# Three chunks of a fused convolution-plus-MLP kernel fed by a pre-turned copy of the input instead of transposes on TensorE, with three smaller moves in the same schedule

## The chip, the cores and the metric

The kernel runs on one core of a Trainium2 chip. The metric is device time in microseconds (us), as a median over runs. A profiled execution gives the trace: five engines (TensorE, called PE for its matmuls and PEld for its weight loads; VectorE, DVE; ScalarE, ACT; GpSimd, POOL; SyncE, SP, which only issues DMAs), each of which runs its own instructions in program order and waits on semaphores, and the DMA queues. SP and ACT issue DMAs through hardware queues, GpSimd through a software queue.

## What is computed

The input is one sequence of 2048 rows and 448 columns. All is in 32-bit floats.

```python
xn  = layernorm(q)                                  # per row
# branch A: a gated long convolution
k_s = sum over t of shift(k, t) * shift_k[:, 3 - t] # 4 taps, per column
kv  = k_s * v
y   = causal_conv(kv, ssm_k) + kv * ssm_D           # 2048 taps per column, by FFT
# branch B: an MLP
h   = xn @ w1 + b1                                  # 448 -> 1792
out = q + xn * y + mish(h) @ w2                     # 1792 -> 448
```

## The kernel before

**Precision by splitting.** Every float operand of the MLP is split in two: `hi = round(x)` by a cast on ACT and `lo = x - hi` by a subtraction on DVE. Each product is then three matmuls (hi*hi, hi*lo, lo*hi) at the fast matmul rate.

**MLP slots.** The 2048 rows are 8 chunks (`NCHUNK`) of 256 rows; the 1792 hidden columns are 7 pairs of 128 (`NP`). There are 56 (chunk, pair) steps `i`, and every step has two slots. In slot 2i PE does `g1_mm(i)` (L444: 22 matmuls of 256 columns). In slot 2i+1 ACT and DVE do `mish(i)` (L460: two activations, then the split into `ach`, `acl`), and PE does `g2_mm(i-2)` (L472: 12 matmuls of 448 columns). Chunk c begins in slot 14c. `g2_evac` (L486) adds the finished chunk to its rows of q and stores them.

**What feeds a chunk.** `g1_mm` needs the normalized rows with the 448 columns on partitions. For chunk c+1 this is made while chunk c runs: `ln_load` (L363) loads q, `ln_stats` (L400) takes mean and variance on DVE, the power -0.5 on POOL and `xn = (q - mean) * rstd` on POOL (on DVE for chunks 0 and 7); `ln_T` (L421) has PE turn xn with four 128x128 transposes for each half chunk, against an identity matrix, into a PSUM tile; `x_split` (L413) makes the two halves `XH` (ACT) and `XL` (DVE). The halves come in slots 2(7c+5)+1 and 2(7c+6) of the chunk before. The xn tile has one buffer. Statistics are put in a list, `drip`, from which one item is taken after most DVE operations (`dv`).

**The convolution** is a two-step FFT by matmuls, dealt out over the same slots by a plan that is written out by hand (`at(slot, ...)` runs ahead of the slot's MLP work, `after(slot, ...)` behind it, L91 to L95).
- Slots 1 to 60: `f1_mm` (L118: 16 matmuls in row and column tiles) for 8 groups of the filter h (`H_AT`; one group, `H_HEAD`, goes in slot 1) and 8 groups of kv (`KV_AT`). It needs both buffers of PSUM pool `pc`. `f1_fold` (L128) empties them with one ACT copy and two DVE operations into an `st` tile (2 buffers), and `f1_out` (L137) has ACT issue two DMAs of `st` to the scratch `Dh` or `Dkv` in DRAM. Ahead of each kv group come four `taps` on DVE (L157; one product on POOL), which end with the product by v (L175).
- Slots 63 to 90: eight octets. `o_load` (L189) loads `ah` from Dh and `av` from Dkv on SP's queue (one buffer each, so each load waits for the matmuls that read the octet before); `h2_mm`, `v2_mm`, `prod`, `i1_mm` transform, multiply and transform back; every one of them needs both `pc` buffers, so the ACT copies of the one before must be done. The load of `av` for octet 0 needs all groups of Dkv to have landed.
- Slots 92 to 112: `e_load`, `fold`, `i2_mm`, `gate`: the last transform and the product with xn. Chunks 6 and 7 (`LATE`) are gated ahead of their MLP sum, the others are added to the output by a DMA.

**The head.** The weights w1 and w2 are loaded and split while chunk 0 runs (`w1_load` L335, `w1_split` L349, `w2_load` L353, `w2_split` L357; raw tiles `kr`, 4 buffers), so that PE takes up each piece soon after it lands. In slot 4 the plan has `f1_mm` of h's group 2 ahead of `g1_mm(2)`, in slot 8 that of group 3. The constant `f1id` holds the first transform's matrix and the identity in one load (L607).

Of the kernel before, what the change touches and what calls it, by code (L numbers as in the profile page):

```python
# [7 lines left out]
F32 = mybir.dt.float32  # L8
# [17 lines left out]
H_AT = {2: 4, 3: 8, 0: 12, 4: 16, 5: 20, 6: 26, 7: 32}  # L26
KV_AT = (24, 29, 34, 39, 44, 50, 55, 60)
# [5 lines left out]
T_LATE = 5  # L33
# [5 lines left out]
def tile_kernel(ctx: ExitStack, tc, q, k, v, sk, hT, sD, w1, b1, w2, c_f1, c_g, c_gi, c_i2, out):  # L39
# [18 lines left out]
    E = dp.tile([NJ * 4, 64, D], F32, name="E")  # L58

    f1id = cp.tile([128, 2, 128], F32, name="f1id")  # L60
    f1, ident = f1id[:, 0], f1id[:, 1]
# [4 lines left out]


# [50 lines left out]
    def f1_mm(src, g, key):  # L118
        x = src.pop(g)
        PS[key, g] = ps = [pc(), pc()]  # L120
        for b in range(2):
            for h in range(2):
                for jj in range(2):
                    rg = 32 * (2 * b + h)
                    nc.tensor.matmul(ps[h][64 * jj:64 * jj + 64, b, :D], f1[rg:rg + 32, 0:64], x[rg:rg + 32, jj],  # L125
                                     start=True, stop=True, tile_position=(rg, 64 * jj))
# [10 lines left out]
    def f1_out(dst, g, key):  # L137
        st = ST.pop((key, g))
        for jj in range(2):
            nc.scalar.dma_start(dst.rearrange("(h p) n d -> p h n d", h=2)[:, :, 4 * g + 2 * jj:4 * g + 2 * jj + 2].rearrange("p h n d -> p h (n d)"),  # L140
                                st[64 * jj:64 * jj + 64].rearrange("p h b d -> p h (b d)"))
# [170 lines left out]
    def gate(c):  # L312
        p = PS.pop(("P", c))
        for jj in range(2):
            j = 2 * c + jj
            r = rstd[:, j:j + 1]
# [44 lines left out]
    XS, XN, turned = {}, {}, []  # L361
# [8 lines left out]

    def ln_parts(c):
        st = mp.tile([128, 2, 6], F32, name="bst", bufs=2)
        ve = mp.tile([128, 2], F32, name="ve", bufs=2)
        xn = mp.tile([128, 2, D + 64], F32, name="xn", tag="xn", bufs=1)
        XN[c] = xn
        eng = nc.gpsimd if 0 < c < NCHUNK - 1 else V

        def stats(jj):
            V.bn_stats(st[:, jj], Q[c][:, jj])

        def aggr(jj):
            V.bn_aggr(mv[:, 2 * c + jj], st[:, jj])

        def eps(a, b):
            V.tensor_scalar(ve[:, a:b], mv[:, 2 * c + a:2 * c + b, 1], EPS, None, op0=ALU.add)  # L385

        def power(a, b):
            nc.gpsimd.tensor_tensor(rstd[:, 2 * c + a:2 * c + b], ve[:, a:b], mhalf[:, a:b], op=ALU.pow)  # L388

        def norm(jj):  # L390
            j = 2 * c + jj
            eng.tensor_scalar(xn[:, jj, :D], Q[c][:, jj], mv[:, j, 0:1], rstd[:, j:j + 1],  # L392
                              op0=ALU.subtract, op1=ALU.mult)

        def tail(a, b):
            eng.tensor_copy(xn[:, a:b, D:], xn[:, a:b, D - 64:D])
# [24 lines left out]
    def ln_T(c, jj):  # L421
# [64 lines left out]
    def g2_evac(c, jjs=(0, 1)):  # L486
# [6 lines left out]
        if not late(c):  # L493
            nc.sync.dma_start(out[:, 2 * c:2 * c + 2], x)

    def mlp_slot(s):
# [3 lines left out]
        if half == 0:  # L500
            if i < n:
                c, p = pairs[i]
                if c + 1 < NCHUNK:
                    if p == 0:
                        ln_load(c + 1)
                    if p == (3 if c in (0, 2, NCHUNK - 2) else 2):
                        ln_stats(c + 1)
# [5 lines left out]
        else:  # L513
            if i < n:
                c, p = pairs[i]
                if p == NP - 2 and c + 1 < NCHUNK:
                    ln_T(c + 1, 0)
# [12 lines left out]
    for g, t in H_AT.items():  # L530
# [8 lines left out]
        at(t + 3, f1_out, Dh, g, "h")  # L539
# [4 lines left out]
    for g, t in enumerate(KV_AT):  # L544
# [9 lines left out]
        at(t + 3, f1_out, Dkv, g, "kv")  # L554
# [34 lines left out]

    at(ts[0] - 7, lambda: dv(len(drip)))  # L590

# [3 lines left out]
    wz = cp.tile([128, NJ], F32, name="wz")  # L595
# [3 lines left out]
    for _ in range(WARM):  # L599
        nc.tensor.matmul(warm[0:NJ, 0:WARM_N], wz, wz[:, 0:1].to_broadcast([128, WARM_N]), start=True, stop=True)  # L600
# [35 lines left out]
    plan.setdefault(4, []).insert(0, (f1_out, (Dh, H_HEAD, "h")))  # L636
    for s in range(nslots):
# [10 lines left out]
        turn()  # L648
# [7 lines left out]
def _constants():  # L656
# [29 lines left out]
    return dict(c_f1=c(np.stack([f1, np.eye(128)], axis=1)), c_g=c(G.reshape(128, 8, 4, 2, 32)), c_gi=c(GI.reshape(128, 8, 2, 2, 64)),  # L686
# [28 lines left out]
```

## Time and profile before

| what | value |
|---|---|
| median of 3 runs | 369.38 us (369.35 to 369.51) |
| profiled execution: its own time | 370.86 us |
| its span, first to last instruction | 368.9 us |
| PE busy | 360.9 us (98%) |
| DVE busy | 262.5 us (71%) |
| ACT busy | 166.3 us (45%) |
| POOL busy | 71.2 us (19%) |
| granted TensorE clock | 1.000 |
| DMA | 79.35 MB, mean 215 GB/s |

The profiled execution's time is 1.96 us more than its span (what lies ahead of the first and behind the last instruction) and 1.48 us more than the median. A row of the timeline reads: start, duration, engine, line, operation, tile written<-tiles read, count, and in brackets the idle time of the engine ahead of it with what ended that time. Rows of a group (by line and form) give the busy time, the mean duration of one in ns, and the idle time ahead. The ends of matmuls are modelled: what PE really took for one is read from start to start.

### The profile page before, as it was taken

To read this page: it belongs to the slowest core of one execution; us is meant where nothing else is said; L and a number is where in the kernel's file an instruction comes from. 1 tells how busy PE (TensorE), PEld (TensorE's weight loads), DVE (VectorE), ACT (ScalarE), POOL (GpSimd) and SP (SyncE) were. 2 spreads that over 40 slices of the span, in tenths; PEclk is the share of its full clock that TensorE was granted. 3 is DMA by queue.
4 is the path that set the end of the run, shared out by engine and by line. 5 is a ranking of instruction groups with operands and counts; after the bars stand their busy time and mean duration, and the time that the engine had idled before them with its cause. 6 is when DMAs were issued, how large, how long until landed. Compare 5 with 4: busy or idle time off the path is not lost.

```text
span 368.9 us, 7464 instructions
## 1 busy us (share of the span) xinstructions
PE 360.9 (98%) x3128; PEld 292.6 (79%) x3128; DVE 262.5 (71%) x359; ACT 166.3 (45%) x277; POOL 71.2 (19%) x58
## 2 busy tenths in 40 slices
PE   7998999999999999999999999999999999999995
PEld 2697888978888989889868666666666889889885
DVE  5897858999998888996515657656385752897751
ACT  3757543344241443253254555556655533235450
POOL 2005000920228222611006000060000005102020
PEclk9999999999999999999999999999999999999999
DMA  7998996839496329514675598896694375949655
GB/s 241 346 285 312 358 368 184 256 105 295 105 299 214 89 66 274 170 48 101 225 244 174 194 261 238 282 301 189 209 292 125 95 248 205 419 195 276 116 66 133
DMA packets 32354, 79.35 MB, mean 215 GB/s; under 512 B 2881, under 2 KB 19138, under 8 KB 32322
## 3 DMA queue, kind: packets, MB, share of 16 engines
q1 hardware_dynamic: 20210, 44.09, 35.8%
q10 hardware_dynamic: 9776, 22.88, 22.2%
q0 software_dynamic: 2336, 11.93, 11.3%
q8 instruction: 24, 0.39, 0.4%
q14 instruction: 8, 0.07, 0.1%
HBM read 50.44 MB, written 28.44 MB: 214 GB/s over the span
## 4 chain that ended last, share of the span: by engine, by line
PE 71%; DMA 12%; DVE 9%; POOL 3%; ACT 2%; issue 2%; SPq 0%; ACTq 0%; POOLq 0%; DVEq 0%
PE pg L457 27%; PE pg L482 10%; PE pg L484 9%; PE pg L483 9%; PE pc L208 7%; DMA kr<-in_w_dram 6%; PE pc L251 4%; PE pc L125 2%; PE pc L308 2%; DMA Dh<-st 2%; DVE x L172 2%; PE pg L407 2%; POOL xn L392 2%; DMA Dkv<-st 1%; DMA av<-Dkv 1%
## 5 line engine op out<-in xcount | busy, mean ns | idle before, releaser
L465 ACT ACTIVATE a<-pg,b1t 128x256 f32<-128x256 f32 x112 | 47.1, 472 | 113.0 <-PE pg L457 88.2
L457 PE MATMUL pg<-XH,w1h 128*128 128x256 f32 x448 | 91.3, 285 | 0.9 <-ACT XH L419 0.9
L75 DVE TENSOR_TENSOR acl<-a,ach 128x512 fp32r<-128x512 f32 x56 | 38.8, 693 | 65.0 <-ACT ach L74 64.7
L457 PEld LDWEIGHTS pg<-XH,w1h 128*128 128x128 f32 x448 | 69.6, 188 | 18.9 <-issue 15.7
L482 PE MATMUL pg<-w2h,ach 128*128 128x448 f32 x224 | 83.1, 371 | 0.0
L483 PE MATMUL pg<-w2l,ach 128*128 128x448 f32 x224 | 81.3, 363 | 0.9 <-DVE w2l L75 0.9
L484 PE MATMUL pg<-w2h,acl 128*128 128x448 f32 x224 | 81.4, 363 | 0.0
L457 PE MATMUL pg<-XL,w1h 128*128 128x256 f32 x448 | 69.6, 277 | 0.2 <-DVE XL L417 0.2
L457 PEld LDWEIGHTS pg<-XL,w1h 128*128 128x128 f32 x448 | 59.4, 188 | 0.4 <-DVE XL L417 0.4
L457 PE MATMUL pg<-XH,w1l 128*128 128x256 f32 x336 | 56.8, 277 | 0.0
L482 PEld LDWEIGHTS pg<-w2h,ach 128*128 128x128 f32 x224 | 42.0, 188 | 11.7 <-issue 9.4
L457 PEld LDWEIGHTS pg<-XH,w1l 128*128 128x128 f32 x336 | 46.8, 188 | 0.0
L483 PEld LDWEIGHTS pg<-w2l,ach 128*128 128x128 f32 x224 | 42.1, 188 | 3.6 <-DVE w2l L75 1.2
L484 PEld LDWEIGHTS pg<-w2h,acl 128*128 128x128 f32 x224 | 42.1, 188 | 2.5
L388 POOL TENSOR_TENSOR rstd<-ve,mhalf 128x2 f32<-128x2 f32 (+1 forms) x9 | 8.8, 977 | 156.2 <-DVE ve L385 156.1
L74 ACT CAST ach<-a 128x512 fp32r<-128x512 f32 x56 | 34.7, 620 | 1.8
L155 POOL TENSOR_TENSOR x<-kr,skb 128x896 f32<-128x896 f32 x8 | 17.1, 2133 | 83.6 <-DVE x L154 62.4
L392 POOL TENSOR_SCALAR xn<-qt,mv,rstd 128x448 f32<-128x448 f32 x12 | 27.8, 2320 | 0.6
L172 DVE TENSOR_TENSOR x<-x 128x896 f32<-128x896 f32 x24 | 26.8, 1115 | 1.4 <-POOL x L155 0.9
L131 ACT COPY st<-pc 128x896 f32<-128x896 f32 x16 | 14.5, 906 | 14.5 <-PE pc L125 12.6
L132 DVE TENSOR_TENSOR st<-pc,st 128x896 f32<-128x896 f32 x16 | 17.4, 1088 | 3.6 <-ACT st L131 3.1
L259 ACT COPY qe<-pc 128x896 f32<-128x896 f32 x16 | 13.8, 912 | 11.0 <-PE pc L251 10.8
(70 smaller groups left out, 389.7 us busy)
## 6 DMA issues: line engine op xcount, KB each, us to landing
Dh<-st ACTq DMA_DIRECT2D x16, 448.0 KB, 6.4
Dkv<-st ACTq DMA_DIRECT2D x16, 448.0 KB, 5.1
ah<-Dh SPq DMA_DIRECT2D x8, 896.0 KB, 7.0
av<-Dkv SPq DMA_DIRECT2D x8, 896.0 KB, 6.2
E<-qe ACTq DMA_DIRECT2D x16, 448.0 KB, 5.2
e<-E POOLq DMA_DIRECT2D x8, 896.0 KB, 7.9
kr<-in_k_dram SPq DMA_DIRECT2D x10, 448.0 KB, 6.7
x<-in_v_dram SPq DMA_DIRECT2D x8, 448.0 KB, 5.2
```

The source lines that it names most:

```text
L74: nc.scalar.copy(h, raw)
L75: V.tensor_sub(l, raw, h)
L132: V.tensor_add(st[:, 0], e, st[:, 1])
L155: nc.gpsimd.tensor_mul(o, KR[g - u // 2], skb[:, u:u + 1].to_broadcast([128, 2, D]))
L172: V.tensor_add(KV[g], KV[g], o)
L208: nc.tensor.matmul(p[32 * t:32 * t + 32, r, :D], g[rs, t, c], a[rs, t], start=True, stop=True, tile_position=(64 * r, 32 * t))
L392: eng.tensor_scalar(xn[:, jj, :D], Q[c][:, jj], mv[:, j, 0:1], rstd[:, j:j + 1], op0=ALU.subtract, op1=ALU.mult)
L457: nc.tensor.matmul(ps[:, n], l, r, start=n_ == 0, stop=n_ == len(mm) - 1)
L465: nc.scalar.activation(a[:, n], ps[:, n], AF.Mish, bias=b1t[:, 2 * p + n:2 * p + n + 1])
L482: nc.tensor.matmul(ps, ah[:, n, cs], w2h[:, f], start=f == 0, stop=False)
L483: nc.tensor.matmul(ps, ah[:, n, cs], w2l[:, f], start=False, stop=False)
L484: nc.tensor.matmul(ps, al[:, n, cs], w2h[:, f], start=False, stop=f == NF - 1)
```

## The change

For chunks 5 to 7 (`NT` = 5 on) the host hands in a second copy of q, `qT`, with columns on partitions. Its 512 KB a chunk are loaded straight into the xn tile. Mean and rstd are taken from the row layout as before (rstd now overwrites the variance in `mv`); POOL stores the 256 pairs (mean, rstd) of a chunk to a DRAM tile `MR`; SP loads them back for each half chunk as one row spread over all 128 partitions, into `idr`, a tile of one buffer which held the identity; DVE subtracts the means and multiplies by rstd along the free dimension, two operations a half chunk; then the split as before, with SBUF as the source. The 24 transposes of these chunks, and POOL's (DVE's for chunk 7) normalizations of them, are gone. `NT_AT` gives the slots, counted from slot 14(c-1) (57 for c = 5).

The rest: the last kv group's `f1_mm` goes from slot 60 to 59, its store from 63 to 61, and the first load of `ah` from ahead of slot 61 to behind slot 59; h's groups 2 and 3 go one slot later (5 and 9), and the stores of groups 1, 2 and 3 are issued by GpSimd instead of ACT; the output store of chunks 0 to 5 is issued behind the next slot (`g2_out`); `f1` and the identity are two loads, the identity (64 KB) first, f1 (32 KB, half of the old columns) behind h's first group; the statistics' tail does norm and tail of a half chunk before the other half's.

```diff
-H_AT = {2: 4, 3: 8, 0: 12, 4: 16, 5: 20, 6: 26, 7: 32}
-KV_AT = (24, 29, 34, 39, 44, 50, 55, 60)
+H_AT = {2: 5, 3: 9, 0: 12, 4: 16, 5: 20, 6: 26, 7: 32}
+KV_AT = (24, 29, 34, 39, 44, 50, 55, 59)
 POOL_H = {20: (0, 2)}
 H0_AT = 63
 OCT_AT = (65, 3)
 I2_AT = {98: (6, 7), 102: (0, 1), 106: (2, 3), 110: (4, 5)}
 LATE = 2
-T_LATE = 5
+NT = 5
+NT_AT = {"q": -5, "x": -1, "stats": -2, "flush": 0, "row": (4, 8), "norm": (7, 10), "split": (8, 11)}
...
+    MR = {c: dp.tile([2, CH], F32, name="MR") for c in range(NT, NCHUNK)}
+
+    f1 = cp.tile([128, 64], F32, name="f1")
+    idr = cp.tile([128, CH], F32, name="idr")
+    ident = idr[:, 0:128]
...
+    def rs(c):
+        return rstd[:, 2 * c:2 * c + 2] if c < NT else mv[:, 2 * c:2 * c + 2, 1]
...
-    def f1_out(dst, g, key):
+    def f1_out(dst, g, key, eng=nc.scalar):
         st = ST.pop((key, g))
         for jj in range(2):
-            nc.scalar.dma_start(dst.rearrange("(h p) n d -> p h n d", h=2)[:, :, 4 * g + 2 * jj:4 * g + 2 * jj + 2].rearrange("p h n d -> p h (n d)"),
+            eng.dma_start(dst.rearrange("(h p) n d -> p h n d", h=2)[:, :, 4 * g + 2 * jj:4 * g + 2 * jj + 2].rearrange("p h n d -> p h (n d)"),
...
+    def xn_tile():
+        return mp.tile([128, 4, CH], F32, name="xn", bufs=1)
...
+        if c < NT:
+            XN[c] = xn = xn_tile().rearrange("p a b -> p (a b)").rearrange("p (j d) -> p j d", j=2)
         eng = nc.gpsimd if 0 < c < NCHUNK - 1 else V
...
-                     lambda: [f(*a) for f, *a in ((power, 0, 2), (norm, 0), (norm, 1), (tail, 0, 2))]])
+                     lambda: [f(*a) for f, *a in ((power, 0, 2), (norm, 0), (tail, 0, 1), (norm, 1), (tail, 1, 2))]])
+
+    def xT_load(c):
+        XN[c] = xn_tile()
+        nc.sync.dma_start(XN[c], qT[c])
+
+    def nt_stats(c):
+        stats, aggr, eps, power, norm, tail = ln_parts(c)
+        drip.extend([lambda: stats(0), lambda: stats(1), lambda: aggr(0), lambda: aggr(1),
+                     lambda: (eps(0, 2), power(0, 2), nt_store(c))])
+
+    def nt_store(c):
+        nc.gpsimd.dma_start(MR[c].rearrange("j (p t) -> p j t", t=2), mv[:, 2 * c:2 * c + 2])
+
+    def nt_row(c, jj):
+        nc.sync.dma_start(idr, MR[c][jj].partition_broadcast(128))
+
+    def nt_norm(c, jj):
+        x = XN[c][:, :, 128 * jj:128 * jj + 128]
+        for t, op in enumerate((ALU.subtract, ALU.mult)):
+            m = idr.rearrange("p (a t) -> p t a", t=2)[:, t:t + 1].to_broadcast([128, 4, 128])
+            V.tensor_tensor(x, x, m, op=op)
+            dv()
+
+    def nt_split(c, jj):
+        if jj == 0:
+            x_tiles(c)
+        x, h, l = (t[:, :, 128 * jj:128 * jj + 128] for t in (XN[c], *XS[c]))
+        nc.scalar.copy(h, x)
+        V.tensor_sub(l, x, h)
+        dv()
...
-        def halves():
-            for lo in range(2):
-                x_split(c, jj, p, lo)
-
-        turned.append(halves)
-        if c < T_LATE:
-            turn()
-
-    def turn():
-        while turned:
-            turned.pop()()
+        for lo in range(2):
+            x_split(c, jj, p, lo)
...
-        if not late(c):
-            nc.sync.dma_start(out[:, 2 * c:2 * c + 2], x)
+
+    def g2_out(c):
+        nc.sync.dma_start(out[:, 2 * c:2 * c + 2], Q[c])
...
-                if c + 1 < NCHUNK:
+                if c + 1 < NT:
                     if p == 0:
                         ln_load(c + 1)
-                    if p == (3 if c in (0, 2, NCHUNK - 2) else 2):
+                    if p == (3 if c in (0, 2) else 2):
...
-        at(t + 3, f1_out, Dh, g, "h")
+        at(t + 3, f1_out, Dh, g, "h", nc.gpsimd if t < 12 else nc.scalar)
...
-        at(t + 3, f1_out, Dkv, g, "kv")
+        at(t + (3 if g < NO - 1 else 2), f1_out, Dkv, g, "kv")
...
-        at(h - d if o else h - 2, o_load, AH, Dh, o, "ah")
+        (at if o else after)(h - d if o else h - 4, o_load, AH, Dh, o, "ah")
...
+    for c in range(NT, NCHUNK):
+        b = 2 * NP * (c - 1) + (1 if c == NT else 0)
+        at(b + NT_AT["q"], ln_load, c)
+        at(b + NT_AT["x"], xT_load, c)
+        at(b + NT_AT["stats"], nt_stats, c)
+        at(b + NT_AT["flush"], lambda: dv(len(drip)))
+        for jj in range(2):
+            at(b + NT_AT["row"][jj], nt_row, c, jj)
+            after(b + NT_AT["norm"][jj], nt_norm, c, jj)
+            after(b + NT_AT["split"][jj], nt_split, c, jj)
+
     at(ts[0] - 7, lambda: dv(len(drip)))
+    for c in range(NCHUNK - LATE):
+        after(2 * (NP * (c + 1) + G2_LAG) + 1, g2_out, c)
...
-    nc.scalar.dma_start(f1id, c_f1)
+    nc.scalar.dma_start(ident, c_id)
...
     h_load(H_HEAD, nc.scalar)
+    nc.scalar.dma_start(f1, c_f1)
...
-    plan.setdefault(4, []).insert(0, (f1_out, (Dh, H_HEAD, "h")))
+    plan.setdefault(4, []).insert(0, (f1_out, (Dh, H_HEAD, "h", nc.gpsimd)))
...
+    rows = np.concatenate([np.arange(D), np.arange(384, D)]).reshape(4, 128)
+    turn = lambda x: x.reshape(128, NCHUNK, 2, D)[..., rows].transpose(1, 4, 3, 2, 0).reshape(NCHUNK, 128, 4, CH)
...
```

Lines that are only "..." stand for what is left out of the diff; what is left out are the removed list `turned`, the renamed constants on the host and a narrower tile for the warm-up matmuls.

More of the change, by code (lines that the diff above doesn't have):

```diff
@@ L38, in tile_kernel @@
 @with_exitstack
-def tile_kernel(ctx: ExitStack, tc, q, k, v, sk, hT, sD, w1, b1, w2, c_f1, c_g, c_gi, c_i2, out):
+def tile_kernel(ctx: ExitStack, tc, q, qT, k, v, sk, hT, sD, w1, b1, w2, c_f1, c_id, c_g, c_gi, c_i2, out):
     nc = tc.nc
@@ L124, in f1_mm @@
                     rg = 32 * (2 * b + h)
-                    nc.tensor.matmul(ps[h][64 * jj:64 * jj + 64, b, :D], f1[rg:rg + 32, 0:64], x[rg:rg + 32, jj],
+                    nc.tensor.matmul(ps[h][64 * jj:64 * jj + 64, b, :D], f1[rg:rg + 32], x[rg:rg + 32, jj],
                                      start=True, stop=True, tile_position=(rg, 64 * jj))
@@ L315, in gate @@
             j = 2 * c + jj
-            r = rstd[:, j:j + 1]
+            r = rs(c)[:, jj:jj + 1]
             x = (Q if late(c) else QA)[c][:, jj]
@@ L387, in power @@
         def power(a, b):
[L388 removed]
+            nc.gpsimd.tensor_tensor(rs(c)[:, a:b], ve[:, a:b], mhalf[:, a:b], op=ALU.pow)
         def norm(jj):
             j = 2 * c + jj
[L392 removed]
+            eng.tensor_scalar(xn[:, jj, :D], Q[c][:, jj], mv[:, j, 0:1], rs(c)[:, jj:jj + 1],
                               op0=ALU.subtract, op1=ALU.mult)
@@ L515, in mlp_slot @@
                 c, p = pairs[i]
-                if p == NP - 2 and c + 1 < NCHUNK:
+                if p == NP - 2 and c + 1 < NT:
                     ln_T(c + 1, 0)
@@ L594, in tile_kernel @@
     V.memset(one, 1.0)
-    wz = cp.tile([128, NJ], F32, name="wz")
+    wz = cp.tile([128, 8], F32, name="wz")
     V.memset(wz, 0.0)
@@ L599, in tile_kernel @@
     for _ in range(WARM):
-        nc.tensor.matmul(warm[0:NJ, 0:WARM_N], wz, wz[:, 0:1].to_broadcast([128, WARM_N]), start=True, stop=True)
+        nc.tensor.matmul(warm[0:8, 0:WARM_N], wz, wz[:, 0:1].to_broadcast([128, WARM_N]), start=True, stop=True)
     nc.scalar.activation(ve0, mhalf, AF.Mish)
@@ L647, in tile_kernel @@
                 fn(*args)
-        turn()
         for fn, args in fns:
```

10 lines of the change are left out of this document (3 added, 7 removed).

## The prediction, made before the changed kernel had run

> **What bounds the kernel now.** I read the page's busy times first, then busy time by stage, then PE's timeline by its starts.
>
> ```profile
> PE 360.9 (98%) x3128; PEld 292.6 (79%) x3128; DVE 262.5 (71%) x359; ACT 166.3 (45%) x277; POOL 71.2 (19%) x58
> ```
> ```profile
> 34.00:365.00 331.00, 330.37 (x2925) 271.16 (x2923) 237.06 (x314) 146.14 (x246) 63.52 (x47) 1.00 0.68 207
> 65.00:100.00 35.00, 35.00 (x278) 30.31 (x278) 34.23 (x44) 13.29 (x24) 12.15 (x7) 1.00 0.63 185
> 200.00:310.00 110.00, 110.00 (x1173) 79.27 (x1166) 64.84 (x80) 58.30 (x88) 9.49 (x9) 1.00 0.71 211
> ```
>
> Columns of the stages: stretch, length, busy PE, PEld, DVE, ACT, POOL, granted clock, DMA share, GB/s. From 34 to 365 us PE is busy 330.37 of 331.00 us at a granted clock of 1.00. So PE sets the end: what leaves its queue shortens the run, unless a new wait appears on PE. Work added elsewhere costs nothing while PE does not wait for it. DVE is full from 65 to 100 (34.23 of 35) and has 45 us free from 200 to 310.
>
> Busy time hides PE's waits in the head, because a stalled matmul's end is modelled; starts show them.
>
> ```profile
> 15.63 1.04 ACT L340 CAST w1h<-kr 128x1024 fp32r<-128x1024 f32 x1 [1.25 <-DMA kr<-in_w_dram]
> 15.70 1.98 PE L125 MATMUL pc<-x,f1id 32*64 32x448 f32 x16
> ...
> 17.61 0.62 PE L457 MATMUL pg<-XH,w1h 128*128 128x256 f32 x3
> 17.70 0.42 DVE L347 TENSOR_TENSOR w1h<-kr,w1h 64x256 fp32r<-64x256 f32 x1
> ...
> 20.30 0.37 PE L482 MATMUL pg<-w2h,ach 128*128 128x448 f32 x1
> ...
> 23.67 5.35 ACTq L140 DMA_DIRECT2D Dh<-st  x2
> ```
> ```profile
> 31.43 1.38 DVE L75 TENSOR_TENSOR w2l<-kr,w2h 128x896 fp32r<-128x896 f32 x1
> 31.45 0.47 PE L482 MATMUL pg<-w2h,ach 128*128 128x448 f32 x1
> ...
> 32.87 0.47 PE L483 MATMUL pg<-w2l,ach 128*128 128x448 f32 x1 [0.94 <-DVE w2l L75]
> ...
> 35.19 0.51 PE L457 MATMUL pg<-XH,w1h 128*128 128x256 f32 x3
> ```
> ```profile
> 20.06 8.35 DMA kr<-in_w_dram
> ...
> 35.35 2.51 PE pg L457 x22
> ...
> 40.71 0.94 PE pc L125 x16
> ```
>
> Three things stand here. ACT is held in its queue from 23.67 to 29.02 by two stores of h's group 2, so the w2 piece that landed at 28.41 is split late, and PE waits for it from 31.45 to 32.87. The first transform of group 2 takes 15.70 to 17.61, twice the 0.94 that such a block takes. And w1's third piece reaches ACT only at 15.63.
>
> **The change part by part.** *Transposes.* 24 of 64 go, in six blocks of four.
>
> ```profile
> L407 PE MATMUL pg<-f1id,xn 128*128 128x128 f32 x64 | 10.3, 281 | 0.8 <-DVE xn L392 0.4 <-POOL xn L396 0.3
> ```
> ```profile
> 304.63 0.62 PE L457 MATMUL pg<-XL,w1h 128*128 128x256 f32 x4
> 305.08 0.36 PE L482 MATMUL pg<-w2h,ach 128*128 128x448 f32 x1
> 305.28 0.36 PE L483 MATMUL pg<-w2l,ach 128*128 128x448 f32 x1
> ...
> 309.54 0.62 PE L457 MATMUL pg<-XL,w1h 128*128 128x256 f32 x4
> ...
> 310.64 0.37 PE L483 MATMUL pg<-w2l,ach 128*128 128x448 f32 x1
> ```
> ```profile
> 193.37 0.47 PE L482 MATMUL pg<-w2h,ach 128*128 128x448 f32 x1
> 193.68 0.36 PE L483 MATMUL pg<-w2l,ach 128*128 128x448 f32 x1
> ...
> 200.15 0.65 PE L407 MATMUL pg<-f1id,xn 128*128 128x128 f32 x4
> ...
> 200.85 0.37 PE L483 MATMUL pg<-w2l,ach 128*128 128x448 f32 x1
> ```
>
> Behind a plain block: from the last L457 group to the second matmul of L483 is 0.65 us without (304.63 to 305.28) and 1.10 us with transposes (309.54 to 310.64): 0.45 us. Behind a block of the convolution it is 0.31 (193.37 to 193.68) against 0.70 (200.15 to 200.85): 0.39 us, since part hides in the change of tiling. Chunk 7's two blocks are of the first kind, chunks 5 and 6 have four of the second: 2 x 0.45 + 4 x 0.39 = 2.46 us. The 281 ns of the group's row is not the price: these overlap. The Trainium skill ("TensorE: Matmul & The Clock Gate", Part 4: PE-mode transpose) gives some 275 ns for one transpose in a kernel's context; the row's 281 agrees as a latency, and an estimate by it would be 24 x 0.275 = 6.6 us and a time of 360.8. The starts speak against it.
>
> *What replaces them.* Per half chunk DVE gets two operations of 128x512, a kind whose nearest row is
>
> ```profile
> L75 DVE TENSOR_TENSOR acl<-a,ach 128x512 fp32r<-128x512 f32 x56 | 38.8, 693 | 65.0 <-ACT ach L74 64.7
> ah<-Dh SPq DMA_DIRECT2D x8, 896.0 KB, 7.0
> ```
>
> 0.69 us each. The strided operand is not in the trace: between 0.69 and double that, and I take 0.69. That is 12 x 0.69 = 8.3 us on DVE (16.6 at the bound), inside the 45 us that DVE has free from 200 to 310; the ACT cast and the DVE subtraction stay. I cost it at nothing. Nor does the trace show the 8-byte stores or the spread rows. Their landing I bound by nothing and by 8 us (somewhat over the 7.0 of the 896 KB loads), and take 7: a slot is 3.6 us here (L483 at 193.68 in slot 65, at 200.85 in slot 67), a row is asked for two or three slots ahead of its use, and PE needs the chunk two or three slots after that. SP issues them in order: the second row waits for DVE's first normalization, and `xT_load` for the split before; behind both stand the loads of `ah` and `av`, which themselves wait for PE's matmuls of the octet before, later than either. So at zero, with PE waiting for the excess if a row is late.
>
> *Head.* With GpSimd issuing, ACT is free at 23.67. It can split the w2 piece at 28.4, and DVE has its low half by 30.5, before PE asks: the 1.2 us wait (1.42 from 31.45 to 32.87 less 0.20) goes. Moving group 2's block from slot 4 to 5 does not give its extra 0.97 us: without it PE meets w1's third piece, whose last part is ready at 17.70 + 0.42 = 18.12. Then 16 of the 22 matmuls are left, 16 x 2.51/22 = 1.83, so `g1_mm(2)` ends at 19.95 against 20.30. Now group 2's block (0.94) follows, then three g2 (12 x 0.20 = 2.41 each), two g1 (2.51) and group 3's block (0.94): 19.95 + 0.94 + 7.23 + 5.02 + 0.94 = 34.08 where 35.19 stood. The head gives 1.1 us. The smaller load at the very front (64 KB less ahead of w1) I bound by 0.3 either way, since the head waits for DMA, and take nothing.
>
> *GpSimd's queue.* Group 2's stores now stand behind chunk 1's normalization there.
>
> ```profile
> 33.09 0.75 POOL L396 COPY xn<-xn 128x128 f32<-128x128 f32 x1
> ```
> ```profile
> 42.76 0.92 ACT L131 COPY st<-pc 128x896 f32<-128x896 f32 x1
> ```
>
> They start at 33.84 instead of 23.67. The `st` tile that they hold is wanted again by group 0's copy at 42.76, about 41.6 then. A group's two stores are 896 KB; at the 7.0 us of the `ah` row and some 1 us of issue they land near 42: a tie on ACT. Nothing, bounded by 0 and 1.5 us.
>
> *The norm order and the seam.*
>
> ```profile
> L392 POOL TENSOR_SCALAR xn<-qt,mv,rstd 128x448 f32<-128x448 f32 x12 | 27.8, 2320 | 0.6
> ```
> ```profile
> 118.39 0.55 PE L407 MATMUL pg<-f1id,xn 128*128 128x128 f32 x3
> ...
> 119.60 0.36 PE L483 MATMUL pg<-w2l,ach 128*128 128x448 f32 x1
> ```
> ```profile
> 191.70 0.61 PE L208 MATMUL pc<-av,g 64*32 64x448 f32 x8 [0.34 <-DMA av<-Dkv]
> ```
> ```profile
> 146.89 1.09 DVE L162 TENSOR_TENSOR x<-kr,skb 128x896 f32<-128x896 f32 x1 [1.68 <-DMA kr<-in_k_dram]
> ...
> 170.46 1.09 DVE L175 TENSOR_TENSOR x<-x 128x896 f32<-128x896 f32 x1
> ...
> 178.93 0.62 DVE L379 BATCH_NORM_STATS2 bst<-qt 128x6 f32<-128x448 f32 x1
> ```
> ```profile
> 173.36 0.36 PE L482 MATMUL pg<-w2h,ach 128*128 128x448 f32 x1
> ...
> 175.86 1.01 PE L125 MATMUL pc<-x,f1id 32*64 32x448 f32 x16
> ```
>
> Chunk 3's transposes wait for POOL's tail: 1.21 us from 118.39 to 119.60 against 0.70 elsewhere. With the first tail ahead of the other half's norm (2.3 us) the 0.5 us go. The first `av` comes 0.34 us late. The last kv block moves from 175.86 to 173.36, and chunk 5's statistics leave the middle of its fold (178.93), so its stores go some 2 us earlier and the 0.34 goes; next in line there is PE's own order. The price is cover: the last kv tile was ready at 171.55 (170.46 + 1.09), 4.3 us early. Now PE asks at 173.36, and DVE has some 1.4 us of statistics ahead of it: 172.95, 0.4 us early. The 1.68 us in which DVE waited for k, whose load stood behind a blocked output store on SP, shrinks too, since that store now comes later. Taken at zero, bounded by 1.5 us.
>
> **The sum** against the span of 368.9: 2.46 + 1.1 + 0.5 + 0.34 = 4.4 us. The profiled execution would go from 370.86 to 366.5, the median, 1.48 lower, from 369.38 to **365.0**.
>
> **The rivals.**
> 1. *DVE becomes late at the last kv group.* For it: 0.4 us of cover, on an engine that is full for long stretches. Against: the k load comes sooner. PE waits by what DVE lacks, 1 us: 366.0.
> 2. *GpSimd's stores come late.* ACT waits at 42 for `st`, w2 pieces are split late and PE stalls again, so that the head's 1.1 and perhaps 0.2 more are lost: 366.3. The Trainium skill ("SBUF — State Buffer", SBUF: two separate sides) says that a GpSimd-issued DMA cannot write its descriptors while DVE holds the shared port in a two-port mode. No run here shows it yet; DVE's work there is nearly all two-input subtractions, which that page does not count among such modes.
> 3. *The chunks come late all the same.* The transposes' time returns as PE's wait for `XH` at the chunks' starts: 365.0 + 2.46 = 367.4. Against: ready two slots ahead by my count.
> 4. *Slower than before.* The second row of a half chunk is late; DVE stands in its queue for it, ACT behind DVE at the cast, and the copies that empty `pc` behind ACT, so PE stands. A row asked for in slot 65 has four slots (14.4 us) until `pc` must be free, less 2.8 us for four operations of 0.69: from 11.6 us of landing each us costs one us per chunk, and the gain is gone at 4.4/3 = 1.5 us more, 13.1 us. At 14 us the time is 365.0 + 3 x 2.4 = 372.2. Against: the stage's large loads take 7.0 us.
>
> **How the numbers follow.** Forecast 0.60, rival 1 0.13, rival 2 0.13, rival 3 0.06, rival 4 0.06, and 0.02 that it is the same for reasons I do not see. The range takes in the head's and the front's upside (363.5: 0.3 of the front, and 1.2 of the 1.5 us in which PE still waits for w1's third piece and what follows it, from 15.70 on) and rivals 1 and 2 at their bounds of 1.5 (366.5) and half a us where both come: 363.5 to 367.0; rivals 3, 4 and the rest are left out. Within 0.2% (0.74 us, about what a measurement of this kernel can tell from no change) comes from the last case, and from 0.02 of rival 3 with more lost than its price: faster 0.90, same 0.04, slower 0.06.
>
> **What would show it.** Right: 40 transposes; L457 to L483 at 0.65 us or less throughout chunks 4 to 6; `g1_mm(5)` near 34.1; no wait of PE near 31, 118 and 191. Wrong: PE idle in front of the last kv block (rival 1), ACT waiting for a `Dh` store at 42 (rival 2), PE waiting for `XH` or `XL` at a chunk's start (rival 3), DVE waiting for `idr` with ACT copies of `pc` behind it (rival 4).

## The result, and the profile after

The changed kernel takes 369.52 us, the kernel before 369.42 us (22 runs each): a ratio of 0.9996, 95% interval 0.9978 to 1.0014. That is no change, where 365.0 us and a range of 363.5 to 367.0 were forecast. The profiled execution took 370.36 us with a span of 368.5 us, against 370.86 and 368.9.

The page's line of busy time and two rows of the groups of the changed kernel say that the change does what it says.

```profile
PE 358.9 (97%) x3104; PEld 291.7 (79%) x3104; DVE 268.1 (73%) x368; ACT 166.6 (45%) x277; POOL 71.0 (19%) x65
```
```profile
L433 DVE TENSOR_TENSOR xn<-xn,idr 128x512 f32<-128x512 f32 x12 | 8.3, 689 | 0.3
L446 PE MATMUL pg<-idr,xn 128*128 128x128 f32 x40 | 6.2, 279 | 1.0 <-DVE xn L401 1.0
```

40 transposes are left of 64, and the two DVE operations that replace each block take 0.69 us each with their strided operand, the lower bound that the forecast took. PE has 2.0 us less to do and the span is 0.4 us shorter, so PE stands still for longer. Where, is seen by setting each matmul of g1 (L486, formerly L457) beside the same one of before and writing down where the difference in start changes:

| place | start after less start before changes by | what stands there |
|---|---|---|
| up to pair 5 (slot 10) | +1.39 us | the head |
| slot 14 to 16 | +0.81 | PE waits for a w2 piece, below |
| slot 40 | -0.52 | order of norm and tail |
| slot 54 | +0.44 | `XL` late, below |
| slot 60 | +0.11 | the kv visit half a step sooner |
| slot 66 | -0.41 | the seam |
| slots 68, 82, 96 | -0.80, -0.80, -0.82 | transposes of chunks 5, 6, 7 |
| slot 74 | +0.33 | PE waits for `hs`, below |

(Changes of under 0.1 us are left out. PE's last matmul starts 0.15 us sooner than in before; the rest of the 0.4 us comes behind it.) The timeline of PE in the changed kernel's head:

```profile
9.32 0.62 PE L486 MATMUL pg<-XH,w1h 128*128 128x256 f32 x3 [1.54 <-ACT XH L458]
10.58 1.22 PE L486 MATMUL pg<-XL,w1h 128*128 128x256 f32 x4 [0.18 <-DVE XL L456]
...
17.64 0.58 PE L486 MATMUL pg<-XH,w1h 128*128 128x256 f32 x3
19.57 0.62 PE L486 MATMUL pg<-XH,w1l 128*128 128x256 f32 x3 [1.35 <-DVE w1l L351]
...
36.58 0.52 PE L486 MATMUL pg<-XH,w1h 128*128 128x256 f32 x3
```

The first g1 starts at 9.32 instead of 8.79, after 1.54 us without work. Four matmuls then take 1.22 us, where four took 0.74 before. At 17.64 PE starts pair 2 and stands until 19.57 for the low part of w1's third piece. Pair 5 starts at 36.58; 35.19 was before, 34.08 was forecast. Busy time by stretch (busy PE is the third column, the granted clock the third from the end) shows what the four matmuls met:

```profile
7.03:10.44 3.41, 1.70 (x11) 1.30 (x11) 2.24 (x5) 2.21 (x4) 0.00 (x0) 1.00 1.01 373
10.44:13.85 3.41, 3.27 (x15) 3.27 (x15) 2.22 (x5) 1.04 (x1) 0.00 (x0) 0.50 0.92 306
13.85:17.27 3.42, 3.42 (x37) 2.57 (x37) 1.52 (x2) 3.04 (x5) 0.00 (x0) 1.00 0.99 390
```

For one stretch of 3.41 us TensorE was granted half its clock, right behind a stretch of the same length in which PE was busy for only 1.70 us. Pair 0 started 0.53 us late and ended 1.96 us late: 1.43 us are the clock's (from the start of pair 0 to that of pair 1 it took 5.62 us; in before 4.12). In before the clock stayed at 1.00 from 4.88 on.

The timeline of the changed kernel around the second `st` wait:

```profile
37.74 2.47 POOL L146 DMA_DIRECT2D Dh<-st  x4
...
47.06 0.91 ACT L137 COPY st<-pc 128x896 f32<-128x896 f32 x1 [2.72 <-DMA Dh<-st]
...
51.87 0.47 PE L512 MATMUL pg<-w2l,ach 128*128 128x448 f32 x1 [0.54 <-DVE w2l L81]
```

This is rival 2 of the prediction: GpSimd issues four stores behind chunk 1's normalization, ACT waits for the tile, and PE for the w2 piece that ACT splits after it. The other steps stand as forecast: no wait of PE near 31, 118 and 191, the matmuls L511 and L512 behind the convolution's block start 0.31 us apart, and DVE has the last kv tile ready at 174.67 where PE asks at 175.82.

```profile
173.58 1.09 DVE L181 TENSOR_TENSOR x<-x 128x896 f32<-128x896 f32 x1
...
175.82 1.01 PE L131 MATMUL pc<-x,f 32*64 32x448 f32 x16
...
202.20 0.47 PE L511 MATMUL pg<-w2h,ach 128*128 128x448 f32 x1
202.51 0.36 PE L512 MATMUL pg<-w2l,ach 128*128 128x448 f32 x1
```

### The profile page after: what moved, and what is told of

Its sections match the earlier page's. It is cut to its first block, busy times and chain, and to the rows that moved or that the text cites. A ratio compares the mean times of both kernels' runs of the same rounds, so it can differ in the third digit from the quotient of the medians.

```text
span 368.5 us, 7457 instructions
## 1 busy us (share of the span) xinstructions
PE 358.9 (97%) x3104; PEld 291.7 (79%) x3104; DVE 268.1 (73%) x368; ACT 166.6 (45%) x277; POOL 71.0 (19%) x65
## 4 chain that ended last, share of the span: by engine, by line
PE 53%; DVE 2%; ACT 1%; ACTq 1%; issue 0%
PE pg L486 20%; PE pg L511 7%; PE pc L214 7%; PE pg L513 7%; PE pg L512 7%; PE pc L257 4%; PE pc L314 2%; ACTq L268 1%; DVE x L178 1%; PE pc L131 1%; DVE x L181 0%; ACT qe L265 0%; ACT a L494 0%; ACT hs L225 0%; DVE qt L518 0%
## 5 line engine op out<-in xcount | busy, mean ns | idle before, releaser
L486 PE MATMUL pg<-XH,w1h 128*128 128x256 f32 x448 | 91.6, 286 | 1.7 <-ACT XH L458 1.5
L486 PEld LDWEIGHTS pg<-XH,w1h 128*128 128x128 f32 x448 | 70.3, 189 | 19.5 <-issue 16.5
L511 PE MATMUL pg<-w2h,ach 128*128 128x448 f32 x224 | 83.3, 372 | 0.0
L512 PE MATMUL pg<-w2l,ach 128*128 128x448 f32 x224 | 81.3, 363 | 0.5 <-DVE w2l L81 0.5
L486 PE MATMUL pg<-XL,w1h 128*128 128x256 f32 x448 | 70.5, 280 | 0.2 <-DVE XL L456 0.2
L486 PEld LDWEIGHTS pg<-XL,w1h 128*128 128x128 f32 x448 | 60.3, 190 | 0.4 <-DVE XL L456 0.4
L486 PE MATMUL pg<-XH,w1l 128*128 128x256 f32 x336 | 57.3, 279 | 1.4 <-DVE w1l L351 1.4
L511 PEld LDWEIGHTS pg<-w2h,ach 128*128 128x128 f32 x224 | 42.0, 187 | 15.1 <-issue 12.2
L486 PEld LDWEIGHTS pg<-XH,w1l 128*128 128x128 f32 x336 | 47.2, 189 | 1.6 <-DVE w1l L351 1.6
L512 PEld LDWEIGHTS pg<-w2l,ach 128*128 128x128 f32 x224 | 42.1, 188 | 3.2 <-DVE w2l L81 0.8
L397 POOL TENSOR_TENSOR mv<-ve,mhalf 128x2 f32<-128x2 f32 x3 | 3.7, 1249 | 97.9 <-DVE ve L394 97.9
L401 POOL TENSOR_SCALAR xn<-qt,mv,rstd 128x448 f32<-128x448 f32 x8 | 20.7, 2591 | 0.4
```

Source lines behind the costliest of these rows:

```text
L486: nc.tensor.matmul(ps[:, n], l, r, start=n_ == 0, stop=n_ == len(mm) - 1)
L511: nc.tensor.matmul(ps, ah[:, n, cs], w2h[:, f], start=f == 0, stop=False)
L512: nc.tensor.matmul(ps, ah[:, n, cs], w2l[:, f], start=False, stop=False)
```

## The experiments

Theory A: the transposes, the norm order and the seam bring what was forecast, and the head eats it. Rival B: what replaces the transposes eats it, in a place that the starts do not show.

**1. The head of before in the changed kernel.**

```
-H_AT = {2: 5, 3: 9,             +H_AT = {2: 4, 3: 8,
-nc.scalar.dma_start(ident, c_id) ... nc.scalar.dma_start(f1, c_f1)
+nc.scalar.dma_start(idr, c_f1)          # one load, f1 and identity
-f1_out(..., nc.gpsimd)          +f1_out(...)
```

> The changed kernel with its head put back as it was before: one load of f1 and identity together at the front, h's groups 2 and 3 at slots 4 and 8, their stores on ACT, warming matmuls of 16 columns; the rest of the change stays (chunks 5 to 7 without transposes, kv visit at 59, the order of norm and tail). Theory A (the head gives back what the rest gains): PE's starts moved forward by 2.42 (transposes), 0.52 (norm order) and 0.41 us (seam), 3.35 us in all, less the 0.44 and 0.33 us of new waits at slots 54 and 74: 2.6 to 3.4 us faster than before, 366.0 to 366.8 against 369.4. Rival B (what replaces the transposes costs what they cost, somewhere the starts do not show): within 0.9 us of before, 368.5 to 369.4.

Measured: 367.45 us, ratio 0.9949 (0.9924 to 0.9973). Theory A: without the new head the change is a gain, though of 2.0 us and not of 2.6 or more. Its timeline:

```profile
33.82 0.51 PE L485 MATMUL pg<-XH,w1h 128*128 128x256 f32 x3
...
274.01 4.49 ACTq L267 DMA_DIRECT2D E<-qe  x2
...
280.89 1.79 PE L213 MATMUL pc<-av,g 64*32 64x448 f32 x32 [1.71 <-ACT hs L224]
```

Two things were not expected. Pair 5 starts at 33.82 with the old head and its stores on ACT: the 1.2 us wait near 31 that the forecast meant to remove is absent. And ACT is held for 4.49 us at two stores of `E`, so that PE stands for 1.71 us at 280.89.

**2. The new head alone, on the kernel before.** The edit is the reverse of the one above, on the old kernel.

> The kernel before with only the head of the change: the front loads in two, h's groups 2 and 3 at slots 5 and 9, their stores on GpSimd, warming matmuls of 8 columns; transposes, kv visit and norm order as before. Theory A (the head costs): slower than before by 1.5 to 2.5 us, 370.9 to 371.9. The forecast's head term: 1.1 us faster, 368.3. Rival B: within 0.5 us of before.

Measured: 372.59 us, ratio 1.0084 (1.0053 to 1.0116). The head alone costs 3.1 us, more than theory A expected, and its interval is far from the forecast's gain of 1.1. Half the clock stands in its profile too, at another place:

```profile
15.49:18.90 3.41, 2.05 (x15) 1.59 (x14) 3.19 (x5) 2.99 (x5) 1.46 (x2) 1.00 0.69 248
18.90:22.31 3.41, 3.41 (x23) 2.95 (x29) 2.58 (x4) 1.65 (x4) 0.00 (x0) 0.50 0.87 207
```

**3. Only the loads, only the stores put back.**

```
(a) -nc.scalar.dma_start(ident, c_id) ... (f1, c_f1)   +nc.scalar.dma_start(idr, c_f1)
(b) -f1_out(..., nc.gpsimd)                            +f1_out(...)
```

> The changed kernel with only the loads at the front put back: f1 and identity come in one DMA ahead of w1 instead of two, everything else changed. Theory A1 (the second small load pushes w1's first pieces back by 0.5 us, PE idles longer and its clock drops to 0.5 from 10.44 for 3.4 us): the clock stays at 1.00 in the head, g1 of pair 5 starts near 34.5 to 35 instead of 36.58, and the time falls by 1.5 to 2.1 us to some 367.4 to 367.9. Rival A2 (the head's loss is that of GpSimd's stores): at most 0.5 us less than the changed kernel, 369.0 to 369.5.

> The changed kernel with only the stores of h's groups 1, 2, 3 put back on ACT's queue. By the trace of the changed kernel the copy of group 0 waits 2.72 us on ACT for the store that GpSimd issued, and PE 0.7 us at 51.87: theory A1 (the loads are the larger part) expects 0.2 to 0.8 us less than the changed kernel, 368.7 to 369.3, with ACT held near 24 us as before; rival A2 (GpSimd's stores are what eats the gain) 1.5 us less or more, 368.0 and under.

Measured: (a) 368.73 us, 0.9984 (0.9964 to 1.0003); (b) 368.15 us, 0.9973 (0.9954 to 0.9993). Neither fits either theory in size, and both intervals overlap that of the changed kernel. In (a) the clock stays at 1.00, but pair 5 starts at 35.08: PE still waits at pair 2 (1.54 us from 16.44). In (b) more came back than the 0.7 us of one profile. By their medians each is a part of the loss, which these runs alone do not show; the wait at pair 2, left over in (a), points at the moved slots as a third.

**4. The kernel before, profiled again.**

> The kernel before, unchanged, profiled a second time. Theory C (PE's wait from 31.45 to 32.87 belonged to the one profiled execution, 370.86 us against a median of 369.4, and not to the kernel): ACT is held for less than 3 us at its store of group 2, no wait of PE near 31, g1 of pair 5 near 33.9 instead of 35.19, span near 367.5. Rival (the forecast's reading: ACT's stores cause it every time): ACT held 5 us again, PE waiting 1.2 us near 31, g1 of pair 5 near 35.2.

Measured: 371.05 us, with a span of 369.1 and pair 5 at 35.55, so not the shorter run that theory C expected. The wait at 31 is gone, and another has come:

```profile
18.55 2.18 ACTq L140 DMA_DIRECT2D Dh<-st  x1
...
27.17 0.48 PE L483 MATMUL pg<-w2l,ach 128*128 128x448 f32 x1 [1.35 <-DVE w2l L75]
```

Both readings are half right. The mechanism is real: a store holds ACT, a w2 piece is split late, PE waits 1.2 us in one profile and 1.5 in the other. But the place moves with the DMAs, and both executions (370.86 and 371.05 us) lie 1.5 us or more above the median of 369.4. The median run does not have this wait, as far as a time without a profile can say.

**5. Only the slots moved, on the kernel of experiment 1.**

```
-H_AT = {2: 4, 3: 8,             +H_AT = {2: 5, 3: 9,
```

> The kernel with the head undone (367.45 us), with only h's groups 2 and 3 moved to slots 5 and 9 again; loads and stores of the head stay as before. Theory (moving the block uncovers PE's wait for w1's third piece, which the block in slot 4 filled): PE waits 0.8 to 1.2 us near 17, g1 of pair 5 starts 0.7 to 1.1 us later than in the kernel with the head undone (33.82), and the median is 368.2 to 368.6. Forecast: 0.1 us, 367.5.

Measured: 369.97 us, 0.9997 (0.9971 to 1.0023). Pair 5 started at 34.61 instead of 33.82, the 0.8 us of the theory. The median is 1.4 us above the theory's range. In the profiled execution (371.65 us) the rest is not the slots' own: ACT was held for 5.33 us at two stores of `E`, PE stood for 2.5 us, and the clock fell to 0.50 behind that. What lengthened the other runs is not shown.

**6. E's stores on GpSimd, on the kernel of experiment 1.**

```
-            nc.scalar.dma_start(E.rearrange(...), qe[...])
+            nc.gpsimd.dma_start(E.rearrange(...), qe[...])
```

> The kernel with the head undone (367.45 us), with the stores of E put on GpSimd instead of ACT, one change. In that kernel's trace ACT was held 3.87 us at 274.63 by one of these stores, its copies of pc came late and PE waited 1.7 us at 280.9. Theory (a store's issue that the DMA queues hold up is paid by ACT and through ACT by PE): no such wait, 0.3 to 1.5 us less, 366.0 to 367.1. Rival (the stores land later from GpSimd and the last stage waits for them): 367.5 or more.

Measured: 366.67 us, 0.9929 (0.9905 to 0.9954). It is the best kernel of the study: its interval lies clear of 1 and of the changed kernel's. Its lead of 0.8 us over experiment 1 is within the two intervals. GpSimd takes the issue, and ACT goes straight on to the copies:

```profile
274.16 1.26 POOL L267 DMA_DIRECT2D E<-qe  x2 [3.56 <-ACT qe L264]
...
276.22 1.71 ACT L224 COPY hs<-pc 128x896 f32<-128x896 f32 x2
```

No wait of PE at slot 74 or behind 270 is left in its trace.

**7. Each part of the head alone, on this best kernel.**

```
(slots)  -H_AT = {2: 4, 3: 8,              +H_AT = {2: 5, 3: 9,
(stores) -f1_out(...)                      +f1_out(..., nc.gpsimd)   # groups 1, 2, 3
(loads)  -nc.scalar.dma_start(idr, c_f1)   +nc.scalar.dma_start(ident, c_id) ... (f1, c_f1)
```

> The best kernel so far (head undone, E's stores on GpSimd, 366.67 us) with only h's groups 2 and 3 moved to slots 5 and 9. Theory (the moved block uncovers PE's wait for w1's third piece, and the wait lets the clock fall in some runs): 1.0 to 1.8 us more, 367.7 to 368.5, g1 of pair 5 near 34.5 to 34.7 instead of 33.70. Forecast: 0.1 us more.

> The best kernel so far (366.67 us) with only the stores of h's groups 1, 2, 3 on GpSimd, at their old slots. Theory (rival 2 of the prediction: the store of group 3 stands behind chunk 1's normalization and ACT's copy of group 0 waits for the tile): ACT waits 1.5 to 3 us for st near 42 to 45, PE 0.3 to 0.8 us near 50, time 0.3 to 0.8 us more, 367.0 to 367.5. Forecast's reading: no loss, and 1.1 us less where ACT was held, 365.6 to 366.7.

> The best kernel so far (366.67 us) with only the front load split in two: the identity at its old place, f1 behind h's first group (and warming matmuls of 8 columns, for want of 32 bytes). Theory (the second small load takes the place in the queue that h's group 2 had, whose load and with it w1's third piece then come half a us or more later): h's group 2 issued near 9.5 instead of 4.7, 0.2 to 0.8 us more, 366.9 to 367.5, and some runs at a lower clock. Forecast: within 0.3 us, 366.4 to 367.0.

Measured: slots 367.29 us, 0.9932 (0.9908 to 0.9956); stores 368.20 us, 0.9967 (0.9941 to 0.9993); loads 368.68 us, 0.9956 (0.9931 to 0.9980). The intervals overlap that of the best kernel, so the times alone do not part these; the traces do. None of the three medians lies in its theory's range: that of slots is 0.4 us below it (and none of its 6 runs had the low clock that was expected in some), that of stores 0.7 and that of loads 1.2 us above. Slots (timeline of PE):

```profile
15.48 0.52 PE L485 MATMUL pg<-XH,w1h 128*128 128x256 f32 x3
17.42 0.62 PE L485 MATMUL pg<-XH,w1l 128*128 128x256 f32 x3 [1.43 <-DVE w1l L350]
...
19.95 1.01 PE L130 MATMUL pc<-x,idr 32*64 32x448 f32 x16
```

PE comes to w1's third piece before it is split, waits, and does group 2's block afterwards instead of meanwhile: pair 5 starts at 34.38 against 33.70, 0.68 us. Stores (timeline, then busy time by stretch):

```profile
45.64 0.91 ACT L136 COPY st<-pc 128x896 f32<-128x896 f32 x1 [4.13 <-DMA Dh<-st]
...
48.83 0.47 PE L510 MATMUL pg<-w2h,ach 128*128 128x448 f32 x1 [0.53 <-ACT w2h L79]
50.45 0.47 PE L511 MATMUL pg<-w2l,ach 128*128 128x448 f32 x1 [1.15 <-DVE w2l L80]
```
```profile
47.70:51.11 3.41, 1.73 (x10) 1.22 (x9) 2.69 (x3) 2.01 (x5) 0.00 (x0) 1.00 1.01 377
51.11:54.52 3.41, 3.41 (x18) 2.56 (x24) 1.79 (x2) 1.37 (x2) 0.00 (x0) 0.50 0.98 267
```

With nothing but the stores moved, ACT waits 4.13 us for `st`, PE 2.1 us in two places (0.69 and 1.42 beyond the usual distance of starts), and half the clock follows: the shift at slot 16 is 3.74 us in this execution, against the 0.81 of the changed kernel. Loads (timeline):

```profile
8.09 0.62 ACT L346 CAST w1h<-kr 128x512 fp32r<-128x512 f32 x1 [5.86 <-DMA kr<-in_w_dram]
9.57 0.33 SPq L117 DMA_DIRECT2D x<-in_hT_dram  x1
9.73 0.62 PE L486 MATMUL pg<-XH,w1h 128*128 128x256 f32 x3 [1.96 <-ACT XH L458]
9.95 0.43 SPq L343 DMA_DIRECT2D kr<-in_w_dram  x1
```

The first half of w1 reaches ACT at 8.09 where it was 6.56 in the best kernel, and group 2's load of h is issued at 9.57 where it was 4.66: the small load of f1 is issued at 4.45 in its stead, and SP's next goes out only when the second half of w1 has landed (9.56). w1's third piece stands behind that load on SP, but goes out at 9.95 instead of 9.84, so the theory's path is not where the time goes: pair 0 starts 1.19 us later than in the best kernel (9.73 against 8.54), and pair 5 is still 1.00 us later (34.70 against 33.70). Over all eighteen profiles pair 0 starts at 8.54 to 9.36 us in the eight with one load (middle 8.8) and at 9.01 to 9.73 in the ten with two (middle 9.4); the ranges overlap.

At full clock the parts add up in the head: 0.68 for the slots, 1.00 for the loads and 0.01 for the stores (pair 5 at 33.71) over 33.70 make 35.39, and the changed kernel's three profiles at full clock, in experiment 8, have pair 5 at 35.00 to 35.49.

**8. What parts the runs of the changed kernel.** Of its 22 runs 12 have a mean clock of 0.995 or less and a median of 370.0 us, 10 have 0.998 or more and 368.1. One stretch of 3.41 us at half clock takes 0.0046 off the mean. Three more profiles of it, then dummy matmuls where PE idles, ahead of pair 0 only and ahead of pairs 0 and 2:

```
+    cover = pc()
+    for _ in range(2):
+        nc.tensor.matmul(cover[0:8, 0, 0:400], wz[:, 0:8], wz[:, 0:1].to_broadcast([128, 400]), ...)
```

> The changed kernel, unchanged, profiled again. Theory (a run is long when one wait of PE leaves a clock window too idle, and the place varies): where the mean clock is 0.995, one window of 3.4 us at 0.5 right behind a wait of PE of 1.4 us or more, at the front (window ending near 10) or near slot 14 to 16 (48 to 52 us), span near 368.2; where it is 0.999 or 1.000, no such window, the same or smaller waits, span near 366.2. Rival (the runs differ by something other than these windows): spans that do not go with the windows, or a window without a wait ahead of it.

> As for the run before it: the changed kernel once more, for the place of its waits and of its clock window.

> As for the two runs before it: the changed kernel once more, for the place of its waits and of its clock window.

> The changed kernel with two matmuls of 400 columns on a tile of zeros between chunk 0's last transpose and the first matmul of pair 0, where PE idled 1.54 us; their output is not used. Theory (in half of the changed kernel's runs the clock drops to 0.5 for one 3.4 us window after this idle time, and those runs are 1.9 us longer): mean clock 0.998 or more in all or nearly all runs, median 368.0 to 368.4 against 369.5 of the changed kernel. Rival (the clock is not what parts the runs): no more runs of high clock than before, median 369.5 or, by delay of the first matmul, more.

> The changed kernel with two matmuls of 400 columns on zeros, their output unused, at both places where PE idles in its head: ahead of pair 0's first matmul and ahead of pair 2's. Theory (the changed kernel's two kinds of runs, 12 of 22 at mean clock 0.995 or less and some 1.9 us longer, come from a clock window that sees too much idle time in these places): no run below 0.997, median 367.6 to 368.3. Rival (the clock falls for another reason): a third or more of the runs below 0.997 and a median near 369.5.

Measured: the three were all of the full-clock kind, 368.15, 368.75 and 368.43 us, with spans of 366.3, 366.9 and 366.6, no stretch at half clock, and pair 5 at 35.21, 35.49 and 35.00. That half of the theory came; none of the three shows the other half. From pair 0 to pair 1 they took 4.10 to 4.16 us, as before did, where the first profile took 5.62. Their waits at pair 2 were 1.4, 1.7 and 1.3 us long, about the 1.5 of the first profile, and PE's idle time ahead of pair 0 was 1.42 to 2.09 us, about the first profile's 1.54 or more, so a wait alone does not bring the clock down. With dummies at one place 2 of 12 runs were below 0.997 and the median 368.74 us, 0.9985 (0.9962 to 1.0007); at both places 1 of 12 and 369.59 us, 0.9993 (0.9966 to 1.0021). Over all kernels with both loads split and slots moved, 28 of 56 runs without dummies had a mean clock below 0.997 and 3 of 24 with them; in the changed family's other kernels (experiments 1, 3a, 5, 6 and 7) it was 12 of 72. So the idle stretches that this head leaves do bring the clock down, in about half of the runs; one load in place of two (experiment 3a, 1 of 12) or two loads with the old slots and stores (experiment 7, 2 of 12) does not do it as often. But both medians lie above their theory's range, and that of the second fill did not fall: it has runs of 369.4 to 370.5 us at full clock, and its one profile (span 365.7) is of the shorter kind. What lengthens those is open.

**9. E's stores on GpSimd in the changed kernel.**

> The changed kernel with only E's stores put on GpSimd. Theory (ACT's hold at E's stores is a loss of the whole family and not of the head): 0.3 to 1.0 us less than the changed kernel, 368.5 to 369.2, and the runs of low clock stay as frequent, since the head is unchanged. Rival (the slow half of the changed kernel's runs is that of ACT held at E's stores): low-clock runs gone and a median of 367.7 or less.

Measured: 369.31 us, 0.9987 (0.9969 to 1.0005), with 7 of 12 runs at the low clock. The low clock goes with the head and not with ACT's hold at `E`; the gain that was expected is within the interval of none. Here the 7 runs of low clock and the 5 of full clock have the same median, 369.3 us, so the clock is not all that parts the runs. In its trace the change at slot 74 is 0.03 us instead of 0.33: that wait was ACT's hold at `E`.

## Why the prediction was wrong

*Transposes, norm order, seam: right.* 2.42 us against 2.46, 0.52 against 0.5, 0.41 against 0.34, each at its place. The seam's figure is partly luck: in the second profile of before PE waited 0.13 us for `av` there and not 0.34, so part of it was that execution's. Rivals 1, 3 and 4 did not come: no wait before the last kv block, `XH` late nowhere in chunks 5 to 7, and no wait of DVE for `idr`.

*The step that failed is the head.* The prediction put 1.1 us of gain there; the starts show 1.39 us of loss in the first profile, a miss of 2.5. It failed in four ways.

1. **The wait at 31.45 was not in every execution.** The profile that shows it lies 1.48 us above the median, the second profile of before has another wait in another place, and two profiles with the same head (experiments 1 and 6) have none. So the median run probably has none either; then the prediction counted its removal as a gain and took the 1.48 off as well, and the same stall was subtracted twice. With one load, old slots and no such wait, pair 5 starts at 33.70 to 33.82. That was the mark to beat, not 35.19.
2. **The moved block was a cover.** In slot 4 group 2's block filled the time in which w1's third piece was split. The prediction saw this and worked out that 16 of 22 matmuls would be left; 19 were, and the block came behind them: 0.7 us.
3. **The smaller front load was not nothing.** It was bounded by 0.3 us either way; pair 0 starts some 0.6 us later with two loads, and with nothing else changed pair 5 was 1.00 us later.
4. **The clock.** No term stood for it. The longer idle time takes TensorE to half its clock for 3.4 us in about half of the runs, 1.43 us in the profile.

Without the fourth, pair 5 starts at 35.0 to 35.5, 1.2 to 1.8 us behind the mark.

*GpSimd's queue at zero: wrong.* The stores went out at 37.74, not 33.84, as the normalization in front of them started later (its power at 31.30, not 28.21) and took longer, and `st` was free at 47.06 instead of 42: PE lost 0.70 us. Rival 2 came true by its wait, though not by the reason that the prediction quotes: nothing shows GpSimd kept from writing descriptors. Its four issues took 2.47 us, 0.62 each, about as long as ACT's (0.58). What held them was the order of GpSimd's queue. The loss is not there in every execution: of the ten profiles with these stores on GpSimd six show it at slot 16 (0.26 to 0.81 us, and 3.74 with the fall of the clock), and of the eight with the stores on ACT none.

*Two small returns.* At slot 54 `XL` is late and PE loses 0.44 us: the split reads a PSUM tile `pg` that PE needs next. The row of POOL in before, then those of POOL, DVE and PE in the changed kernel:

```profile
145.28 0.71 POOL L388 TENSOR_TENSOR rstd<-ve,mhalf 128x2 f32<-128x2 f32 x1 [8.73 <-DVE ve L385]
```
```profile
146.99 1.08 DVE L168 TENSOR_TENSOR x<-kr,skb 128x896 f32<-128x896 f32 x1
147.16 1.49 POOL L397 TENSOR_TENSOR rstd<-ve,mhalf 128x2 f32<-128x2 f32 x1 [8.74 <-DVE ve L394]
...
161.30 0.68 DVE L456 TENSOR_TENSOR XL<-pg,XH 128x512 fp32r<-128x512 f32 x1
...
162.04 0.62 PE L486 MATMUL pg<-XH,w1h 128*128 128x256 f32 x3 [0.20 <-DVE XL L456]
```

The prediction noted that DVE's wait for k would shrink, and booked it as cover. It did shrink, and GpSimd's power now stands beside a DVE operation and takes 1.49 us instead of 0.71; everything behind it on GpSimd is later by that. It is no accident of one execution: this operation takes 1.48 or 1.49 us in all fifteen profiles with this part of the change and 0.71 in the three without. The Trainium skill ("SBUF — State Buffer", SBUF: two separate sides) says that a GpSimd operation that reads SBUF and a DVE operation with two inputs in SBUF exclude each other, for the whole instruction. The trace agrees: DVE ends at 148.07, and GpSimd ends 0.58 us after that. At slot 74 ACT is held at a store of `E` and PE waits; that hold was not in before's trace, and a hold at `E` cost PE 1.7 and 2.5 us in the profiles of experiments 1 and 5.

*The sum.* In the profile 4.4 us were forecast and 0.4 came. The head misses 2.5, slot 16 0.8, slots 54, 60 and 74 0.9: 4.2; small changes, and what lies behind PE's last matmul, make the difference to the 4.0 that are missing. In the median 4.5 are missing. An estimate from the rows: 1.1 that an ordinary run of before did not have to give; 1.2 to 1.8 for the new head at full clock; 1.4 for the clock in about half of the runs, so 0.7; 0 to 0.8 at slot 16; and the 0.9 of slots 54 to 74: 3.9 to 5.3. The other side of the account holds too: with the old head and E's stores on GpSimd, the 2.42, 0.52 and 0.41 less the 0.44 make 2.9 us, and the best kernel's ratio of 0.9929 is 2.6 us (1.7 to 3.5).

What stays open: why two loads of fewer bytes at the front land w1's first half later than one; why single runs at full clock differ by 2 us; and why the ten full-clock runs with the loads alone have a median of 368.6 us, 1.9 above the best kernel, where the trace accounts for 1.0.

## What to carry to other kernels

A stall in one profiled execution that hangs on when DMAs land is not a term of the sum until a second profile shows it; where the profiled execution is above the median by about the size of such a stall, it may be in the difference already. Before moving a block of matmuls, ask which late operand it was covering, and before moving a store to another engine, what stands ahead of it in that queue and who needs its tile next. A gap of PE near half a clock window can cost about its own length again (here 1.43 us).

## What the runs showed of the hardware

The clock comes down on less than an idle window. The Trainium skill ("TensorE: Matmul & The Clock Gate", Part 1: The HAM clock gate) gives a free-running window of 3413 ns and half the clock after an idle one. The window agrees: the stretches at half clock are 3.41 us long here and the first full clock came anywhere from 3.6 to 7.0 us. But the stretches ahead of the five falls in the eighteen profiles had PE busy for 1.18, 1.23, 1.70, 1.73 and 2.05 us of 3.41, none of them idle throughout, while one with 1.67 in the second profile of experiment 8 (the first at full clock there) and one with 1.71 in experiment 1 were followed by full clock:

```profile
5.97:9.38 3.41, 1.67 (x10) 0.85 (x8) 1.48 (x5) 1.30 (x3) 0.34 (x1) 1.00 1.03 371
9.38:12.80 3.42, 2.90 (x22) 2.71 (x22) 3.23 (x6) 1.86 (x3) 0.00 (x0) 1.00 0.93 316
```
```profile
278.87:282.28 3.41, 1.71 (x34) 0.37 (x32) 2.21 (x3) 2.75 (x5) 0.00 (x0) 1.00 0.61 164
282.28:285.69 3.41, 3.41 (x43) 2.81 (x38) 1.57 (x2) 1.98 (x3) 0.00 (x0) 1.00 0.00 0
```

So no sharp border shows, and the same idle time hits in some runs and not in others.

A DMA's issue can hold its engine's queue: 5.35 us on ACT in before, 4.49 and 5.33 at `E`, with other DMAs under way each time. At the front of before SP's next load went out at 9.58, 0.02 us after a piece of w1 had landed, and in the changed kernel at 9.65, 0.01 us after one. The 5.35 us of before are two issues of 0.58 us, and the second goes out at 28.44, where a w2 piece has landed at 28.41. The issue of a store on an engine that also empties PSUM can therefore be a wait that PE pays.
